# The first batch of a fused attention-and-experts kernel: its chain up to the first mixture matmul, reordered over all engines

## The chip, the cores and the metric

The kernel runs on one core of a Trainium2 chip. The metric is the device time of one execution, in microseconds; medians are over several executions. The profile's "span" (first to last instruction) is about 1.8 us shorter than the device time of the same execution. Engines are named as in the profile: PE (TensorE), PEld (its weight loads), DVE (VectorE), ACT (ScalarE), POOL (GpSimd), SP (SyncE, which issues transfers). "Lnnn" is a line of the kernel that is profiled, so the same code has other line numbers before and after.

## The reference

```python
def phi(x):                                   # polynomial sketch, r = 8, x: (4, 4, 1088, 32)
    a = np.einsum('rd,bhsd->bhsr', S1, x)
    b = np.einsum('rd,bhsd->bhsr', S2, x)
    return np.einsum('bhsi,bhsj->bhsij', a, b).reshape(*x.shape[:-1], r * r)
q_p, k_p = phi(q), phi(k)
kv  = np.einsum('bhsf,bhsd->bhfd', k_p, v);  z = k_p.sum(axis=2)
num = np.einsum('bhsf,bhfd->bhsd', q_p, kv)
den = np.einsum('bhsf,bhf->bhs', q_p, z)[..., None] + 1e-06
x   = (num / den).transpose(0, 2, 1, 3).reshape(4352, 128)
# mixture of 4 experts, D = 128, F = 1024
p = domain_probs / (domain_probs.sum(-1, keepdims=True) + 1e-09)
for e in range(4):
    out += p[:, e:e+1] * (np.maximum(x @ w1[e], 0) @ w2[e])
```

S1 and S2 arrive as 64-bit floats, so the kernel decodes them from integer words.

## The kernel before

A batch's keys are turned by DVE (`kT`), projected by PE (`kf`), added and multiplied (`fs`, `kp`), and contracted with v on PE (`kv`). Queries go through `qc`, `qp`, `nd`, `den` to `xT`, the input of the mixture. The mixture is 64 matmuls a chunk: `hp` into `hid` (DVE) into `acc`. Chunks of later batches are prepared in pieces that are laid between mixture steps; only the first chunk has nothing to hide behind. I call the time until the first `hp` the front, and the rest the main part.

```python
# S: 8 small loads, half of them on ACT, into a tile that GpSimd zeroes
nc.gpsimd.memset(s_raw[:, :], 0)
for i, src in enumerate((S1, S2)):
    for c in range(4):
        (nc.sync if i == 0 else nc.scalar).dma_start(...)
kn[0] = load_rows(k, 0, "kn")
...                                    # dp on ACT
vn[0] = load_v(0, (nc.sync, nc.scalar))
qn[0] = load_rows(q, 0, "qn")
...
nc.vector.memset(warm[:, :], 0.0)
for _ in range(10):                    # warm-up matmuls, PE only
    nc.tensor.matmul(wp[:, :], warm[:, 0:P], warm[:, :], start=True, stop=True)
...                                    # decode of S on DVE, 19 operations and a transpose; sk, sq by one operation each

def keys(b):                           # the same code for every batch
    ...
    for h in range(H):
        for x in range(2):
            eng = nc.vector if b == 0 else nc.gpsimd
            eng.tensor_tensor(out=_ap(kp, ...), in0=..., in1=..., op=ALU.mult)
    ...
    for p in range(2):
        for t in range(NT):            # 66 columns: this pair's two heads
            nc.tensor.matmul(kv[:, WP * p : WP * p + WP], kp[0:n, t, p, :],
                             ve[0:n, t, 2 * p : 2 * p + 2].rearrange("p h d -> p (h d)"), ...)

pieces = front()
while not ready:                       # the first chunk's keys, then its queries, one after the other
    next(pieces)
```

## Time and profile before

| | before |
|---|---|
| median device time (4 runs) | 550.57 us (550.18 to 550.66) |
| profiled execution | 548.74 us, span 546.9 us |
| first hp | 30.03 us |
| from the first hp to the end | 516.9 us |
| PE busy | 530.9 us (97%) |

The lines behind this are shown in the prediction. An fp32 matmul appears as two passes, so "kv x36" is 18 matmuls.

### The profile page before, as it was taken

The page shows a single profiled execution, that of the slowest core. Times are in us where ns is not written, and L with a number is a line of the kernel's source. Part 1 is how long each engine was busy: PE and PEld are TensorE (multiplying, and loading weights), DVE is VectorE, ACT ScalarE, POOL GpSimd, SP SyncE. Part 2 cuts the span into 40 slices and gives each one's busy share as a digit, 9 for nine tenths or more (in the row PEclk, how much of TensorE's full clock was granted, in tenths as well). Part 3 has the DMA queues.
Part 4 walks back from the last instruction along what each step waited for, and adds up shares of the span by engine and source line. Part 5 has one row for each costly group of instructions (what it writes and reads, how often), then busy time and mean ns, then how long its engine had stood idle before and what let it go on. Part 6 is the DMA issues. An engine that isn't in the chain of part 4 may idle for free.

```text
span 546.9 us, 5467 instructions
## 1 busy us (share of the span) xinstructions
PE 530.9 (97%) x2102; PEld 370.1 (68%) x2102; DVE 335.3 (61%) x799; ACT 19.5 (4%) x41; POOL 29.4 (5%) x104
## 2 busy tenths in 40 slices
PE   5689999999999999999999999999999999999997
PEld 3578888776676556666766556675667665565997
DVE  6478875377776745357875664437776654554554
ACT  1000000000000000000000000000000000000000
POOL 2100002400000002400000000400000000000000
PEclk8579999999999999999999999999999999999999
DMA  6870412001105102000201000200200100100100
GB/s 192 253 235 0 128 51 68 1 0 29 42 1 141 43 0 73 0 0 1 73 0 56 5 1 1 71 1 0 72 1 0 43 0 0 35 0 0 16 7 7
DMA packets 32970, 22.54 MB, mean 41 GB/s; under 512 B 21296, under 2 KB 29616, under 8 KB 32944
## 3 DMA queue, kind: packets, MB, share of 16 engines
q1 hardware_dynamic: 31584, 21.79, 14.2%
q10 hardware_dynamic: 1360, 0.41, 0.3%
q8 instruction: 16, 0.26, 0.2%
q14 instruction: 10, 0.08, 0.1%
HBM read 19.88 MB, written 2.31 MB: 41 GB/s over the span
## 4 chain that ended last, share of the span: by engine, by line
PE 95%; DVE 3%; issue 0%; DMA 0%; ACTq 0%; ACT 0%; POOL 0%; DVEq 0%; POOLq 0%
PE hp L406 43%; PE acc L422 43%; PE kv L301 4%; PE nd L359 3%; PE qc L331 2%; PE kf L269 1%; DVE den L372 1%; DVE kp L287 0%; DMA s_raw<-in_S_dram 0%; DVE kT L241 0%; ACTq L101 0%; DVE qp L347 0%; DVE fs L274 0%; DVE hid L408 0%; DVE qa L344 0%
## 5 line engine op out<-in xcount | busy, mean ns | idle before, releaser
L408 DVE SCALAR_TENSOR_TENSOR hid<-hp,gate 128x384 f32<-128x384 f32 (+4 forms) x448 | 213.0, 476 | 193.7 <-PE hp L406 189.0
L406 PE MATMUL hp<-xT,w_sb 128*128 128x384 f32 (+4 forms) x896 | 310.1, 428 | 2.9 <-DVE xT L377 2.7
L422 PE MATMUL acc<-hid,w_sb 128*128 128x384 f32 (+4 forms) x896 | 307.7, 425 | 0.0
L406 PEld LDWEIGHTS hp<-xT,w_sb 128*128 128x128 f32 x896 | 165.0, 191 | 75.2 <-DVE xT L377 3.3
L422 PEld LDWEIGHTS acc<-hid,w_sb 128*128 128x128 f32 x896 | 166.1, 190 | 72.9
L287 POOL TENSOR_TENSOR kp<-fs 128x128 f32<-128x128 f32 (+1 forms) x48 | 19.0, 436 | 315.3 <-DVE fs L274 315.3
L372 DVE RECIPROCAL den<-den 128x128 f32<-128x128 f32 (+1 forms) x37 | 32.3, 875 | 1.8 <-ACT den L362 1.8
L347 DVE TENSOR_TENSOR qp<-qa,qb 64x384 f32<-64x384 f32 (+4 forms) x56 | 26.6, 474 | 1.1
L362 ACT ACTIVATE den<-nd,eps 64x384 f32<-64x384 f32 (+4 forms) x28 | 14.4, 515 | 348.6 <-PE nd L359 348.1
L301 PEld LDWEIGHTS kv<-vx,kp 128*128 128x128 f32 x144 | 19.7, 208 | 3.9 <-issue 1.8
L301 PE MATMUL kv<-vx,kp 128*128 128x66 f32 x144 | 20.4, 295 | 1.4 <-DVE fs L274 1.3
L359 PE MATMUL nd<-qp,kvz 128*128 128x384 f32 (+4 forms) x56 | 18.2, 445 | 3.1 <-DVE qp L347 3.1
L359 PEld LDWEIGHTS nd<-qp,kvz 128*128 128x128 f32 x56 | 10.6, 199 | 8.7 <-DVE qp L347 3.6
L269 PEld LDWEIGHTS kf<-sk,kT 128*128 128x128 f32 x72 | 10.9, 217 | 6.0 <-DVE kT L241 3.9
L269 PE MATMUL kf<-sk,kT 128*128 128x128 f32 x72 | 11.2, 305 | 3.0 <-DVE kT L241 3.0
L344 DVE STREAM_SHUFFLE qa<-qf 128x384 f32<-128x384 f32 (+4 forms) x28 | 13.9, 497 | 0.0
L377 DVE TENSOR_TENSOR xT<-nd,den 64x384 f32<-64x384 f32 (+4 forms) x28 | 13.3, 473 | 0.5
L331 PE MATMUL qc<-qT,sq 128*128 128x384 f32 (+4 forms) x28 | 10.6, 462 | 1.0 <-DVE qT L327 1.0
L257 POOL COPY vx<-vn 128x128 f32<-128x128 f32 x32 | 8.3, 312 | 10.9 <-DMA vn<-in_v_dram 10.9
L331 PEld LDWEIGHTS qc<-qT,sq 128*128 128x128 f32 x28 | 5.7, 209 | 3.1 <-issue 1.1
L272 ACT COPY fs<-kf 128x256 f32<-128x256 f32 (+1 forms) x12 | 3.8, 319 | 105.4 <-PE kf L269 105.3
L431 DVE STREAM_TRANSPOSE ob<-acc 128x384 f32<-128x384 f32 (+4 forms) x14 | 6.9, 494 | 0.6 <-PE acc L422 0.6
(56 smaller groups left out, 60.8 us busy)
## 6 DMA issues: line engine op xcount, KB each, us to landing
gate<-gates SPq DMA_DIRECT2D x6, 768.0 KB
w_sb<-in_moe_w_dram SPq DMA_DIRECT2D x8, 512.0 KB
gate<-gates SPq DMA_DIRECT2D x4, 640.0 KB
kn<-in_k_dram SPq DMA_DIRECT2D x4, 544.0 KB
qn<-in_q_dram SPq DMA_DIRECT2D x4, 544.0 KB
vn<-in_v_dram SPq DMA_DIRECT2D x28, 64.0 KB
out_dram<-ob SPq DMA_DIRECT2D x24, 48.0 KB
gate<-gates SPq DMA_DIRECT2D x2, 384.0 KB
```

The lines of the kernel that those rows point to most:

```text
L269: nc.tensor.matmul(kf[:, P * t : P * t + P], kT[:, P * (t0 + t) : P * (t0 + t + 1)], sk[:, :], start=True, stop=True)
L287: eng.tensor_tensor(out=_ap(kp, 0, P, 256 * s0 + P * (h // 2) + 64 * x + 32 * (h % 2), [[256, m], [R, 4], [1, R]]), in0=_ap(fs, 0, P, 64 * ...
L301: nc.tensor.matmul(kv[:, WP * p : WP * p + WP], kp[0:n, t, p, :], ve[0:n, t, 2 * p : 2 * p + 2].rearrange("p h d -> p (h d)"), start=(t == 0),
L331: nc.tensor.matmul(qc[:, 0:n], sq[:, :], qT[:, 0:n], start=True, stop=True)
L344: nc.vector.stream_shuffle(in_=qf[:, 0:n], out=qa[:, 0:n], mask=mask_a[x])
L347: nc.vector.tensor_tensor(out=qp[p][64 * x : 64 * x + 64, 0:n], in0=qa[64 * p : 64 * p + 64, 0:n], in1=qb[64 * p : 64 * p + 64, 0:n], op=A ...
L359: nc.tensor.matmul(nd[p][:, 0:n], kvzs[b][:, p, :], qp[p][:, 0:n], start=True, stop=True)
L362: nc.scalar.activation(den[64 * p : 64 * p + 64, 0:n], nd[p][64 - 64 * p : 128 - 64 * p, 0:n], ACTF.Identity, bias=eps[64 * p : 64 * p + 6 ...
L372: nc.vector.reciprocal(den[:, s : s + w], den[:, s : s + w])
L406: nc.tensor.matmul(hp[:, 0:n], w1_sb[:, e, P * f : P * f + P], xT[chunks[m]][:, 0:n], start=True, stop=True)
L408: nc.vector.scalar_tensor_tensor(out=_ap(hid[i], 0, P, 0, [[32, n // 32], [1, 32]]), in0=_ap(hp, 0, P, 0, [[32, n // 32], [1, 32]]), scala ...
L422: nc.tensor.matmul(acc[m][:, 0:n], w2_sb[:, e, f, :], hid.pop(i)[:, 0:n], start=(kk == 0), stop=(kk == NK - 1))
```

## The change

The intent: shorten the front by sharing its work over the idle engines, start the next batch's keys in it, and keep PE's clock up. The core of the diff:

```diff
-    s_raw = cpool.tile([P, 2 * D], I32, name="s_raw")
-    nc.gpsimd.memset(s_raw[:, :], 0)
-    ... 8 loads
+    s_raw = cpool.tile([32, 2 * D], I32, name="s_raw")
+    nc.vector.memset(s_raw[:, :], 0)
+    for i, (eng, src) in enumerate(((nc.scalar, S1), (nc.sync, S2))):
+        eng.dma_start(s_raw[R * i : R * i + R, :], src.bitcast(I32))
 ...
+    load_weights(0)                              # was behind the gates
     nc.vector.memset(warm[:, :], 0.0)
+    nc.scalar.activation(warm[:, 0:1], warm[:, 1:2], ACTF.Identity)
-    for _ in range(10):
+    for _ in range(13):
 ...   # decode: 18 operations and a transpose, ordered so that few wait for their neighbour
+    for h in range(H):
+        (nc.vector.tensor_copy if h % 2 else nc.scalar.copy)(_ap(sk, 32 * h, ...), _ap(s_T, ...))
+        nc.gpsimd.tensor_copy(_ap(sq, 32 * h, ...), _ap(s_T, ...))
 ...   # value copies: GpSimd, 9 pieces -> ACT, 3 pieces; sum of the gates: DVE -> GpSimd
+    def start():
+        for r in range(3): key_turn(0, r)
+        make_gates()
+        qs = queries(0, 0)
+        next(qs)                                 # turn of q
+        kf = [key_project(b, 0)]
+        kf.append(key_project(b, 1))
+        key_add(b, 0, kf[0])
+        for h in range(H):
+            key_product(b, 0, 4, h, 0, nc.vector)
+            key_product(b, 0, 4, h, 1, nc.gpsimd)
+        ...                                      # third kf, adds, store_gates, second products
+        kn[1] = load_rows(k, 1, "kn")
+        load_gate(0, 0)
+        ...
+        for p in range(2):
+            key_sum(b, p, kv, slice(0, H))       # 132 columns: all four heads
+        for _ in range(9): next(qs)              # query products while kv runs
+        key_divide(b, kv, 0, 256 + 2 * (D + 1))
+        ahead = keys(1)
+        next(qs)                                 # nd, den
+        for _ in range(5): next(ahead)           # batch 1: three turns, eight of nine kf
+        for _ in qs: pass                        # reciprocals, xT
+        return ahead
```

## The prediction

> **What bounds the kernel now.** I read the page's shares and slices first, then the chain of waits over the first 45 us, the timeline of the first 45 us, and last the landing records of the transfers. PE is 97% busy, and the chain that ended last is 95% PE. In the chain of waits:
>
> ```profile
> 2.20 1.58 DMA s_raw<-in_S_dram
> ...
> 7.49 0.29 DVE sk L188
> ...
> 11.47 1.70 DVE kp L287 x8
> ...
> 14.85 5.80 PE kv L301 x28
> 20.68 0.49 DVE kvz L313 x2
> ...
> 27.76 1.37 DVE den L372 x2
> ...
> 30.03 1.65 PE hp L406 x4
> ```
>
> (start us, length us, what.) The first mixture matmul starts at 30.03 us. From there to about 543.5 us the PE digits are 9 and the chain is PE without a break except for one stall of some 2 us near 42 us (reciprocals ahead of hid). So two parts: a serial front of 30.03 us, and 513.5 us in which PE is the bound. The change can gain in the front, by moving PE work into it, and hardly anywhere else. The windows view adds the clock of the front (columns: window, PE, PEld, DVE, ACT, POOL busy, PEclk, DMA share, GB/s):
>
> ```profile
> 15.00:20.00 5.00, 5.00 (x27) 4.69 (x27) 0.65 (x3) 0.00 (x0) 2.60 (x9) 0.60 0.69 165
> 20.00:25.00 5.00, 1.62 (x5) 0.95 (x4) 3.01 (x14) 0.00 (x0) 0.00 (x0) 0.50 0.99 328
> 25.00:30.00 5.00, 1.65 (x4) 1.14 (x4) 2.98 (x7) 0.83 (x2) 0.00 (x0) 0.50 1.03 359
> 30.00:35.00 5.00, 4.97 (x21) 4.79 (x22) 2.96 (x11) 0.00 (x0) 0.00 (x0) 0.69 1.14 333
> ```
>
> PE runs at half clock from 16.0 to 33.1 us, through most of kv, nd and the first hp, although kv kept it "busy" 5.00 of 5 us. A later batch's kv at full clock shows the difference: 18 passes in 2.10 us (117 ns each), against 28 in 5.80 us (207 ns each).
>
> ```profile
> 103.51 2.10 PE kv L301 x18
> ```
>
> The timeline shows what ACT does before its first copy:
>
> ```profile
> 1.19 4.45 PE L137 MATMUL wp<-warm 128*128 128x512 bf16 x10 [1.19 <-DVE warm L116]
> 6.56 1.53 ACTq L88 DMA_DIRECT2D vn<-in_v_dram  x2
> 8.13 1.28 ACT L272 ACT_TABLE_LOAD   x1 [8.13 <-DMA vn<-in_v_dram]
> ```
>
> ACT's queue is held until 8.1 us by v loads that wait for earlier transfers; the table load comes only then. Today nobody notices: its first copy is wanted at 10.3.
>
> **What the Trainium skill says.** "TensorE: Matmul & The Clock Gate", Part 1: the array runs at half rate until a free-running activity window of about 3.4 us was busy, and falls back after an idle one. The trace agrees: its clock records change in steps of 3.413 us. kv at half clock did not count as busy, which fits 66 columns streaming only half of each 207 ns pass (192 columns take 162 ns at full clock, so 66 take 56, and 112 at half). The same Part 1 ("Architectural detail") says ACT and DVE are strict FIFO; the trace agrees, the table load following the last issue at once. "ScalarE: Activation LUTs", What ACT_TABLE_LOAD costs, gives about 1283 ns; the trace has 1283. "GPSIMD Engine Reference", Engine selection, has GpSimd about 2 times slower on two-input work; the trace has 408 ns for a 128x128 kp product there and 1.70/8 = 213 ns on DVE.
>
> **The change, part by part.**
>
> S and the decode. S comes in 2 transfers instead of 8, zeroed by DVE rather than GpSimd. I estimate landing at 2.5 us (the first of the old ones: issued 0.91, landed 2.28) instead of 3.78. The decode is 18 operations in an order where few wait for their neighbour (about 0.10 us apart, as independent ones are now; dependent ones are 0.21 apart) plus transpose: about 2.4 us instead of 3.5. s_T is ready near 5.1 instead of 7.4. kn goes out 0.9 us earlier and lands near 5.7 (now 6.54); kT is ready by 7.3 instead of 9.3.
>
> But this gain is not kept. In the built instruction order ACT has its loads first, then the table load, then a dummy activation that writes one column of the warm tile, then two of the four sk copies. The v loads wait as they do now, 0.9 us earlier: the last issue at 6.85 to 7.2, table load to 8.5, dummy to 8.7, sk to 9.2. And the first warm-up weight load waits for ACT, since it reads the tile that the dummy writes. So the warm-ups, which began at 1.19, begin at 8.75 and stand ahead of kf in PE's order. There are 13: 0.427 us each at half clock (their spacing now), half of that at full, and full comes 2 to 5.4 us later depending on the window's phase, say 3.7. 3.7/0.427 = 8.7 slow ones and 4.3 fast: 4.6 us. **kf starts near 13.4 us, not 8.66.** That is the wait that takes the place of the decode.
>
> From there PE is warm, and everything is shorter. kf: 16 passes at 111 ns (8 took 0.885 warm in a later batch) end at 15.2, with ACT copies of 0.37 and DVE adds of 0.38 behind. Products: half on DVE (4 x 0.213, 4 x 0.246), half on GpSimd (4 x 0.408, 4 x 0.464): adds done 16.8, pt 17.2, DVE's products 18.2, GpSimd's 18.9. The value copies move to ACT in 3 pieces, about 1.6 us, done 17.7. kv starts at 17.0 and does 36 passes; 132 columns at full clock stream 112 ns, so a pass still costs about 115 ns, and PE counts as busy: ends 21.4 with the waits (now 13.65 to 20.64). The query shuffles and products (22.62 to 25.59 now, 3.0 us) run on DVE during kv instead of after it: ready at 21.2. kvz to 22.0, nd 0.65 us.
>
> Then a new piece: DVE turns batch 1's keys (0.69 + 0.69 + 0.2) before the reciprocals. They need kn of batch 1, whose load stands behind the four gates stores on SP; those need pt (17.2) and take 1.8 us to issue. kn is issued at 19.0 and lands 3.6 us later at about 22.6 (estimate from kn's 4.2 now beside other loads). Turns end 24.1, reciprocals 1.37, xT 0.74: **first hp at about 26.2**, 3.8 us earlier. The gate tile follows kn and lands near 24; weights 0 were loaded long before.
>
> Main part. 16 of batch 1's kf passes now run in the front, while DVE does reciprocals: 16 x 0.111 = 1.8 us off PE. If hp starts at full clock, the half-speed start is spared: from 30.03 to 33.17 PE did 1.4 us worth of full-clock work, so up to 1.7; I count 0.9, since it is about even whether the window before hp (kf of batch 1 alone, 1.8 of 3.4 us) holds the clock. DVE has three more adds in the first chunk, where it has little slack: +0.5. The other batches do the same work, with copies on ACT instead of GpSimd, off the path: 0.
>
> Sum: -3.8 - 1.8 - 0.9 + 0.5 = -6.0. I shade this by 0.5 because DVE and GpSimd now multiply at the same time in one memory. **550.5 - 5.5 = 545.0 us.**
>
> **The rivals.**
> 1. The clock falls back before or in kv. For it: gaps near 16 us while PE waits for products. Against: 132 columns, and kf just before. Then kv takes 36 x 0.22 = 7.9 us instead of 4.4, nd 1.7, hp starts cold: 549 to 551, no gain.
> 2. The order of ACT does not hurt: the warm-ups run early, or full clock comes at once. Then kf starts at 9.3 to 12.5 and hp near 23 to 25: 541 to 543. The waits in the built order speak against the first form; the phase allows part of the second.
> 3. A transfer becomes the bound: kn of batch 1 or the gate tile, behind the gates stores, lands 2 to 3 us later than I think. hp near 28.5: 547.
> 4. Giving back in the main part: ACT's value copies block den, or DVE stalls hid more in the first chunk: +1 to +3. Against it: after 45 us PE waits almost nowhere now, and the order after the first chunk is nearly the old one.
>
> **Range and chances.** The phase of the window alone moves the front by -0.9 to +0.9 us and the clock rival by +4; transfers +2; a quicker ACT -3. So 541.5 to 549.0, 8 in 10. Two per cent is 11.0 us: below 539.5 needs hp to start by about 21 us; I give it 0.03. Slower by 11 us needs something broken in the main part: 0.01.
>
> **What would show it.** Right: in the new timeline the table load at 7 to 8.5 on ACT, the warm-ups only after it, the first kf 4 to 5 us later than before; PEclk near 1 through kv; kv passes near 115 ns; DVE waiting for a kn transfer ahead of its turn; hp first at 25 to 27.5 us; 8 kf pairs ahead of it. Wrong: warm-ups at 1 us; PEclk 0.5 through kv; the first hp before 24 or after 28.5; or the time from first hp to the end differing from 513.5 - 2.2 by over 2 us.

## The result

| | before | after |
|---|---|---|
| median device time (4 runs each) | 550.57 us (550.18 to 550.66) | 543.91 us (543.14 to 544.39) |
| profiled span | 546.9 us | 542.6 us |
| first hp | 30.03 us | 28.65 us |
| from the first hp to the end | 516.9 us | 514.0 us |

The ratio is 0.9879 (95% interval 0.9862 to 0.9896). Ratios here are the mean time of one kernel's fast runs over that of the other's of the same rounds, so not quite the ratio of the medians. The change is faster by 1.2%, inside the 2% that counts as the same.

The chain of waits of the changed kernel over the front (start us, length us, what):

```profile
2.45 4.69 DMA vn<-in_v_dram
...
7.16 0.33 ACTq L88
...
9.07 5.73 PE wp L141 x13
14.80 1.07 PE kf L266 x8
...
16.30 0.44 DVE fs L274
...
24.26 0.50 DVE kvz L307 x2
...
28.65 0.61 PE hp L485 x2
```

S and its decode are gone from the chain. In their place stand a load of v that ACT must wait for before it may issue its last one, and then the warm-up matmuls. From the first key add (16.30) to kvz (24.76) the chain is DVE without a gap, and kv is no longer in it; after that come nd on PE, den on ACT, and the reciprocals and xT on DVE. (The piece "kf" begins with kf's second pass. The first, at 14.59, follows the last warm-up; I take first passes where I give kf's start.)

ACT's timeline of the changed kernel (start us, busy us, engine, line, what; in brackets the wait before it):

```profile
5.75 1.74 ACTq L88 DMA_DIRECT2D vn<-in_v_dram  x2
7.51 1.28 ACT L119 ACT_TABLE_LOAD   x1 [7.51 <-DVE dsum L209]
8.81 0.21 ACT L119 ACTIVATE warm<-warm 128x1 bf16<-128x1 bf16 x1
8.92 0.42 ACT L188 COPY sk<-s_T 32x32 f32<-32x32 f32 x2
```

The table load starts 0.02 us after the last issue ended (7.16 + 0.33 = 7.49), so it is the queue and not "DVE dsum" that held it; the name in brackets is the last semaphore event seen, and the table load waits for none. The warm-ups, at 9.07 in the chain above, start 0.05 us after the dummy activation ends (8.81 + 0.21 = 9.02), and kf follows the last warm-up.

The windows view of the changed kernel, with the same columns as in the prediction:

```profile
15.00:20.00 5.00, 3.44 (x28) 3.12 (x26) 3.67 (x11) 2.23 (x6) 2.92 (x7) 1.00 0.01 2
20.00:25.00 5.00, 4.29 (x32) 3.67 (x31) 4.79 (x18) 0.00 (x0) 0.79 (x2) 1.00 0.68 205
25.00:30.00 5.00, 3.42 (x24) 2.93 (x23) 3.88 (x10) 1.58 (x4) 0.00 (x0) 1.00 0.57 115
30.00:35.00 5.00, 4.98 (x30) 4.93 (x31) 3.51 (x13) 1.55 (x4) 4.96 (x13) 1.00 0.96 272
```

PEclk is 1.00 from 15.02 us on, when kf had begun. (It is printed as 1.00 before that as well, but the trace's first clock record is at 15.02 us, and all 13 warm-ups ran 0.427 us apart, that is at half clock: in a_kp_dve below, where the clock rose among them, the last ones are 0.216 us apart.) In the timeline kv's 36 passes take 4.92 us, 0.112 us apart for the most part, against 0.213 us at half clock in the kernel before:

```profile
16.76 1.53 DVE L282 TENSOR_TENSOR kp<-fs 128x128 f32<-128x128 f32 x4
16.80 1.75 POOL L282 TENSOR_TENSOR kp<-fs 128x128 f32<-128x128 f32 x4 [8.87 <-DVE fs L274]
...
18.83 1.96 POOL L282 TENSOR_TENSOR kp<-fs 128x160 f32<-128x160 f32 x4 [0.28 <-DVE fs L274]
18.93 2.04 DVE L282 TENSOR_TENSOR kp<-fs 128x160 f32<-128x160 f32 x4
...
19.17 4.92 PE L294 MATMUL kv<-vx,kp 128*128 128x132 f32 x36
```

A DVE product took 1.53/4 = 382 ns here against 213 ns before: beside each other, the two engines got through one product each per 0.411 us.

### The profile page after: what moved, and what is told of

Its sections match the earlier page's. It is cut to its first block, busy times and chain, and to the rows that moved or that the text cites. A ratio compares the mean times of both kernels' runs of the same rounds, so it can differ in the third digit from the quotient of the medians.

```text
span 542.6 us, 5443 instructions
## 1 busy us (share of the span) xinstructions
PE 525.9 (97%) x2105; PEld 366.1 (67%) x2105; DVE 333.2 (61%) x788; ACT 25.3 (5%) x56; POOL 26.1 (5%) x80
## 4 chain that ended last, share of the span: by engine, by line
PE 95%; DVE 3%; DMA 1%; issue 0%; ACT 0%; ACTq 0%; DVEq 0%
PE hp L485 43%; PE acc L501 43%; PE nd L381 3%; PE kv L294 2%; PE qc L353 1%; PE wp L141 1%; PE kf L266 1%; DMA vn<-in_v_dram 1%; DVE kp L282 1%; DVE den L394 1%; DVE qp L369 0%; DVE fs L274 0%; DVE hid L487 0%; ACT den L384 0%; DVE qa L366 0%
## 5 line engine op out<-in xcount | busy, mean ns | idle before, releaser
L282 POOL TENSOR_TENSOR kp<-fs 128x128 f32<-128x128 f32 (+1 forms) x56 | 22.6, 442 | 316.4 <-DVE fs L274 316.4
L294 PEld LDWEIGHTS kv<-vx,kp 128*128 128x128 f32 x144 | 17.9, 190 | 2.2
L294 PE MATMUL kv<-vx,kp 128*128 128x66 f32 (+1 forms) x144 | 18.5, 277 | 0.0
L141 PE MATMUL wp<-warm 128*128 128x512 bf16 x13 | 5.7, 632 | 9.1 <-ACT warm L119 9.1
L266 PEld LDWEIGHTS kf<-sk,kT 128*128 128x128 f32 x72 | 9.8, 197 | 3.0 <-DVE fs L274 0.8
L266 PE MATMUL kf<-sk,kT 128*128 128x128 f32 x72 | 10.0, 281 | 0.6 <-DVE fs L274 0.5
L141 PEld LDWEIGHTS <-warm 128*128 128x128 bf16 x13 | 1.8, 146 | 12.1 <-ACT warm L119 9.1
L349 DVE STREAM_TRANSPOSE qT<-qn 128x384 f32<-128x384 f32 (+4 forms) x14 | 6.9, 493 | 3.9 <-DMA qn<-in_q_dram 3.9
```

The source lines that it names most:

```text
L266: nc.tensor.matmul(kf[:, P * t : P * t + P], kT[:, P * (t0 + t) : P * (t0 + t + 1)], sk[:, :], start=True, stop=True)
L282: eng.tensor_tensor(out=_ap(kps[b], 0, P, 256 * t0 + P * (h // 2) + 64 * x + 32 * (h % 2), [[256, n], [R, 4], [1, R]]), in0=_ap(fss[b], 0, ...
L294: nc.tensor.matmul(kv[:, 256 * p : 256 * p + heads.stop * (D + 1) - heads.start * (D + 1)], kps[b][0:n, t, p, :], ve[0:n, t, heads].rearra ...
```

## The experiments

Twelve runs were made, all correct; two are of the kernel before and one of the changed kernel, unchanged. The table gives their medians, the kernel before in the same rounds, the ratio, and from the profiled execution the first hp and the time from there to the end of the span. "Clock" is the mean granted clock of the profiled execution; it counts the time before the trace's first clock record as full, so the 1.000 of the changed kernel leaves out its warm-ups at half clock. The change's other parts (value copies on ACT, gate sums on GpSimd, S in two loads) had no run of their own.

| run | us | before | ratio | first hp | hp to end | clock |
|---|---|---|---|---|---|---|
| changed kernel, first measured | 543.91 | 550.57 | 0.9879 | 28.65 | 514.0 | 1.000 |
| b_again | 549.77 | 551.36 | 0.9983 | 29.46 | 517.6 | 0.983 |
| a_kv66 | 546.17 | 551.36 | 0.9908 | 30.65 | 514.1 | 0.989 |
| b_kv132 | 549.08 | 551.36 | 0.9954 | 27.98 | 517.3 | 0.986 |
| a_warm_free | 540.74 | 551.36 | 0.9808 | 23.93 | 513.9 | 0.997 |
| a_old_decode | 543.95 | 550.39 | 0.9894 | 28.11 | 513.9 | 1.000 |
| a_kp_dve | 543.36 | 550.39 | 0.9881 | 27.14 | 514.0 | 1.000 |
| a_no_ahead | 546.70 | 550.39 | 0.9945 | 27.19 | 517.4 | 0.994 |
| c_early_act | 536.97 | 550.39 | 0.9771 | 20.92 | 513.9 | 1.000 |
| a_again | 543.29 | 550.46 | 0.9864 | 28.53 | 514.0 | 1.000 |
| b_look | 550.17 | 550.46 | – | 31.34 | 517.1 | 0.978 |
| a_warm8 | 542.71 | 550.46 | 0.9853 | 27.18 | 513.9 | 0.999 |
| d_qc_mid | 540.44 | 550.46 | 0.9811 | 24.01 | 515.6 | 0.991 |

The column "hp to end" is the most useful one: it has a floor of 513.9 to 514.1 us, whatever the front took, and each excess over it goes with one or both of two things, told below: batch 1's kf in the main part, and half clock at its start.

**The kernel before against itself.** No edit.

> The kernel before, unchanged, to see its own spread. Its profiled run took 548.74 us, its timed runs 550.2 to 550.7; the changed kernel's profiled run lies inside its timed ones. Theory: the phase of PE's activity window differs from run to run, and one more window of 3.41 us at half clock in the front or at the start of the mixture costs up to 1.7 us. Then the runs fall on two or three levels about 1.7 us apart, and the mean granted clock of a run is lower where the time is longer (548.7 went with 0.981; 550.5 should go with about 0.975 to 0.978). Rival: the gap is something else (launch, DMA), and time and clock are unrelated.

Six executions took 548.68, 548.68, 548.85, 550.68, 551.23 and 552.46 us, with clocks of 0.981, 0.981, 0.983, 0.974, 0.975 and 0.972. The order by clock is nearly the order by time, as the theory of the window's phase says, though the levels are not clean steps of 1.7 us, and the two short traces are out of order (17.1 us at half clock with a span of 547.1 us here, 20.5 us with 546.9 us in the first profile). (Three of the eleven runs of the kernel before beside them report clock 1.000 with 551.7 to 552.0 us; since the first clock records of a trace can be missing, as above, I make nothing of those.) So a single profile of this kernel is known only to some 3 us. The later look shows what a typical run is like:

> The kernel before once more for its trace, since both traces so far are of its short runs (546.9 and 547.1 us, clock 0.981 and 0.983), while its timed runs have spans of 547 to 550.7. Theory of the window's phase: a trace of span 548.6 or more shows half clock for longer (20 us at 0.972 to 0.978: 24 to 30 us at half), the first hp at 30 to 32 us or half clock for 2 to 3 us more after it, and the same 515.5 to 517.5 from hp on otherwise. If this one is short again, the question stays with the clock figures of the timed runs.

This run took 550.17 us (a single execution, so its state is unknown). Its chain of waits:

```profile
16.29 5.67 PE kv L301 x28
...
26.95 1.66 PE nd L359 x4
...
31.34 1.65 PE hp L406 x4
```

Its clock records show half speed from 7.4 to 14.2 and from 17.6 to 34.7 us. The first hp came at 31.34 us and the rest took 517.1 us, as in the other two traces of this kernel. The theory holds in this trace; the profile that I had predicted from was one of the kernel's short executions.

**kv's width, both ways.**

```diff
 # a_kv66: the changed kernel
-            key_sum(b, p, kv, slice(0, H))
+            key_sum(b, p, kv, slice(2 * p, 2 * p + 2))
-        key_divide(b, kv, 0, 256 + 2 * (D + 1))
+        key_divide(b, kv, 0, 256)
```

> The changed kernel with only kv of the first batch put back to 66 columns a pass. Clock theory: at full clock a 66-column pass streams 56 of 117 ns, so PE no longer counts as busy during kv, the clock falls to half for one window or more around kv and nd, and the first hp starts later or cold: +1 to +4 us, to 545 to 548, mean clock below 1.0. Rival (the front is bound by DVE from the first key add to kvz, with no gap, and kv is beside it; kf and qc keep PE busy enough): within 0.5 us of 543.9, clock 1.0.

546.17 us. Chain and windows of this run:

```profile
18.82 6.41 PE kv L294 x36
...
30.86 0.63 PE hp L485 x2
```

```profile
20.00:25.00 5.00, 5.00 (x27) 4.74 (x25) 3.53 (x14) 0.00 (x0) 0.28 (x1) 0.61 0.77 234
25.00:30.00 5.00, 4.42 (x19) 4.23 (x19) 3.76 (x9) 1.21 (x3) 0.00 (x0) 0.50 0.46 82
```

With 66 columns the clock fell at 21.1 us, in the middle of kv, and stayed at half until 31.3. kv was back in the chain, and nd took 1.65 us instead of 0.61. (The first hp pass is at 30.65; the chain's piece begins with the second.) All four executions had a clock of 0.989 to 0.991. The rival, that kv's width does not matter because kv lies beside DVE's chain, is refuted: without the width the median is some 2 us longer.

```diff
 # b_kv132: the kernel before, first batch only
-                    kv[:, WP * p : WP * p + WP],
+                    kv[:, 256 * p : 256 * p + KW],            # KW = 2 * WP for b == 0
-                    ve[0:n, t, 2 * p : 2 * p + 2]...
+                    ve[0:n, t, (slice(0, H) if b == 0 else slice(2 * p, 2 * p + 2))]...
 ...   # and kvz reads kv at the new places
```

> The kernel before with only kv of its first batch widened to all heads. Clock theory: kv was the bound of the old front (5.0 us in which DVE waited for it) because the clock fell to half in it; with 132 columns the clock stays or comes back: kv 4.2 to 5 us instead of 7.0, and the first hp starts at full clock: -3 to -5 us, 545.5 to 547.5. Rival: a full-width pass at half clock streams 224 ns, longer than the 207 ns of now, and the clock does not come back in time: 0 to +1 us.

549.08 us, a ratio of 0.9954: about half of what I expected. kv itself went as the theory says, 28 passes in 3.99 us:

```profile
15.02 3.99 PE kv L302 x28
...
23.58 1.66 PE nd L360 x4
...
27.98 1.65 PE hp L407 x4
```

But then PE had only the query projection to do while DVE worked through the queries, and the clock fell again at 21.7 us and stayed at half until 31.9, so nd and the start of the mixture were slow as before (517.3 us from hp on). Width keeps the clock only while kv runs; it is the rest of the order that carries it to the mixture.

**The warm-ups' wait for ACT.**

```diff
 # a_warm_free: the changed kernel
-    nc.scalar.activation(warm[:, 0:1], warm[:, 1:2], ACTF.Identity)
+    dummy = cpool.tile([P, 2], F32, name="dummy")
+    nc.vector.memset(dummy[:, :], 0.0)
+    nc.scalar.activation(dummy[:, 0:1], dummy[:, 1:2], ACTF.Identity)
```

> The changed kernel with the dummy activation on a tile of its own, so that the warm-up matmuls no longer wait for ACT. ACT's own order is left, so sk is still ready only at 9.35 us. My step: the warm-ups tied to ACT cost the front what the decode gained. Then warm-ups run at about 1.2 to 6.7, kf starts at 9.4 instead of 14.8, the first key add is held by the turn of q in front of it on DVE until 11.75 (now 16.3), so up to 4.5 us are gained if the clock holds: 539.5 to 541. Rival: the late warm-ups are what keeps the clock; with them early PE goes into kf and kv at half clock (kf 3.7, kv 8 us) and the gain is mostly lost: 543 to 546, mean clock 0.97 to 0.985.

540.74 us. The first key add came at 11.70 us, held by the load of q as foreseen, and the first hp at 23.93 instead of 28.65:

```profile
6.93 4.37 DMA qn<-in_q_dram
11.32 0.38 DVE qT L351
...
23.93 0.61 PE hp L487 x2
```

The clock dipped for one window (8.9 to 12.3 us, while kf ran) and came back. So the tie between warm-ups and ACT costs the changed kernel about 3 us net: it does let kf run at full clock (0.112 us a pass, against 0.213 here), but that is worth less than the wait.

**The decode.** In place of the new 18 operations, the old 19 in the old order, on 32 partitions. (The expectation says 22, which counts the transpose and the making of sk and sq too.)

```diff
 # a_old_decode: the changed kernel
-    expo = bits("expo", high, 1, shl, 21, shr)
-    sign = bits("sign", high, 31, shr, 31, shl)
-    ...
+    sign = bits("sign", high, 31, shr, 31, shl)
+    expo = bits("expo", high, 1, shl, 21, shr)
+    mant = either("mant", bits("mant0", high, 12, shl, 9, shr), bits("mant1", low, 29, shr))
+    ...
```

> The changed kernel with the old decode of S (22 operations in the old order, on 32 partitions). My step: the decode is no longer on the path, since sk waits for ACT until 9.3 us and kf for the warm-ups until 14.8; so s_T comes about 1.2 us later (5.8 instead of 4.6), kT about 1 us later (8.2 instead of 7.2), and nothing else moves: first hp within 0.3 us of 28.65, time within 0.5 us of 543.9. Rival: the shorter decode is part of the gain: +0.8 to +1.2 us.

543.95 us. The transposed S was ready 1.2 us later (its transpose starts at 5.58 instead of 4.38), the keys' turn followed (6.39 instead of 5.75), and the warm-ups and kf did not notice: the first hp at 28.11. The faster decode is worth nothing in this order that these runs can resolve.

**The split of the products.**

```diff
 # a_kp_dve: the changed kernel
-            key_product(b, 0, 4, h, 1, nc.gpsimd)
+            key_product(b, 0, 4, h, 1, nc.vector)
 # and the same for the second group
```

> The changed kernel with all key products of the first batch on DVE, none on GpSimd. Theory: DVE and GpSimd slow each other, so that the half share on DVE (4 in 1.53 us, 4 in 2.04) took almost as long as all eight do alone (1.70 and 1.97 before): products then take 3.7 us instead of 3.5 to 3.6, the front hardly moves (-0.1 to +0.4 us): 543.8 to 544.5. Rival: the DVE products are slow for a reason of their own (the order, the waits) and not because GpSimd runs beside: then eight at 0.38 and 0.51 us take 7.1 us, +3.5 us.

543.36 us. All eight products on DVE took about as long as four did beside GpSimd:

```profile
15.19 1.71 DVE L282 TENSOR_TENSOR kp<-fs 128x128 f32<-128x128 f32 x8
...
17.54 1.93 DVE L282 TENSOR_TENSOR kp<-fs 128x160 f32<-128x160 f32 x8
```

That is 214 and 241 ns each, against 382 and 510 ns in the changed kernel. From the first key add to the end of kvz it is 8.5 us here (14.73 to 23.24) and 8.5 us there (16.30 to 24.75). The rival, that DVE was slow for a reason of its own, would have given 7 us of products; they took 3.6. Sharing them moved work off DVE without moving its end. (The 0.5 us in the median's favour goes with shorter warm-ups, 4.37 us in this profile; from the first key add to hp it is 12.4 us in both kernels.)

**Batch 1's keys in the front.**

```diff
 # a_no_ahead: the changed kernel
-        for _ in range(5):
-            next(ahead)
 ...
-        for _ in range(3):
+        for _ in range(8):
             next(ahead)
             yield
```

> The changed kernel without the five pieces of batch 1's keys (three turns, eight kf) in the front; they come as the first pieces of the mixture. Theory: those pieces are free in the front (they lie in the shadow of ACT's den and of the reciprocals) and take 1.8 us of PE off the mixture: without them +1.8 us, and +0.5 to 1.5 more because DVE is tight in the first chunk: 545.7 to 547.5; first hp at most 0.3 us earlier. Rival: they delay the reciprocals and so cost the front what they save: within 0.5 us of 543.9.

546.70 us. The front was no shorter for it: from the first key add (14.78) to hp (27.19) it took 12.4 us, as in the changed kernel (16.30 to 28.65). The main part took 517.4 us, 3.4 us over the floor. Of these, 16 passes at 111 ns = 1.8 us are batch 1's kf (an estimate). The rest, which I had put down to DVE beforehand, goes with the clock. The windows view:

```profile
25.00:30.00 5.00, 2.81 (x8) 2.49 (x9) 3.69 (x9) 0.00 (x0) 0.00 (x0) 0.55 0.72 185
30.00:35.00 5.00, 5.00 (x30) 5.00 (x30) 1.36 (x6) 0.74 (x2) 0.00 (x0) 0.76 1.05 328
```

Without kf between nd and hp, PE idles for 3 us there, and the mixture starts at half clock, which lasted from 25.5 to 32.4 us. So batch 1's keys in the front are worth 1.8 us as work, and the remaining 1.6 us go with the clock that they hold; no run separates the two further.

**The number of warm-ups.**

```diff
 # a_warm8: the changed kernel
-    for _ in range(13):
+    for _ in range(8):
```

> The changed kernel with 8 warm-up matmuls instead of 13. My step: the warm-ups stand in the way of kf. Then kf starts after 8 x 0.427 = 3.4 us of them, at 12.5 instead of 13.4 to 14.8, and the first hp comes 0.9 to 2.3 us earlier: 541.7 to 543 if kf and kv get full clock soon enough. Rival: 13 are needed for the clock; with 8 the clock rises one window later or falls in the gap before kv, kf takes 3.4 us and kv up to 8: 544 to 548, mean clock below 1.

542.71 us against 543.29 for the changed kernel on the same chip, which ran beside it as follows.

> The changed kernel, unchanged, beside the last variants on one chip. 543.1 to 544.6 us. Its front depends on when full clock comes within the warm-ups (5.73 us of them in the first profile, 4.33 to 5.7 in the variants), so its runs should lie within 1.5 us, and the first hp at 27.1 to 28.7; from the first hp to the end 513.9 us.

Its four runs took 543.06 to 544.26 us. With 8 warm-ups kf started at 12.48 instead of 14.69 us, at half clock, so its first eight passes were 0.213 us apart instead of 0.112; the first hp came 1.35 us earlier in the profiles and the medians differ by 0.6. This is a small gain at the edge of what the spread allows; it agrees in sign with the warm-ups standing in kf's way, and the clock, full from 14.70 us on, did not need all 13.

**ACT out of the way.** This version came out of the above: the dummy activation on its own tile and ahead of ACT's v loads, all sk copies on DVE, and q's turn behind the key adds.

```diff
 # c_early_act: the changed kernel
+    dummy = ...; nc.vector.memset(dummy[:, :], 0.0)
+    nc.scalar.activation(dummy[:, 0:1], dummy[:, 1:2], ACTF.Identity)   # behind the load of dp
 ...
-    nc.scalar.activation(warm[:, 0:1], warm[:, 1:2], ACTF.Identity)
 ...
-        (nc.vector.tensor_copy if h % 2 else nc.scalar.copy)(
+        nc.vector.tensor_copy(
 ...
-        next(qs)                        # in front of the first kf
 ...
         store_gates()
+        next(qs)
```

> The changed kernel with ACT out of the way of the start: the dummy activation on a tile of its own and ahead of ACT's v loads, so that the table load runs at about 2 us; all four sk copies on DVE; the turn of q behind the key adds on DVE. Theory: the front is then warm-ups to 6.7, kf, and DVE's chain of about 8 us from the first key add (now at about 8.4 to 9.5) to kvz, then 4.4 us to hp: first hp at 20.7 to 22.5, time 536.5 to 539, if clock and the kn and gate transfers (kn of batch 1 at about 16.5) allow it. Rivals: the clock falls to half between kf and kv (kv 8 us): 540 to 542, mean clock 0.985 to 0.99; or the later v loads on ACT hold kv or the fs copies: 539 to 541.

536.97 us, ratio 0.9771 (0.9750 to 0.9791): the only run that is faster than the kernel before by the 2% that count. Against the changed kernel's 0.9879 it is 1.1% better, clear of both intervals. ACT's timeline and the chain of waits:

```profile
1.99 1.28 ACT L106 ACT_TABLE_LOAD   x1 [1.99 <-DVE warm L121]
2.06 1.34 ACTq L83 DMA_DIRECT2D vn<-in_v_dram  x3
```

```profile
1.26 5.36 PE wp L143 x13
6.62 1.14 PE kf L268 x8
...
11.86 4.65 PE kv L296 x36
...
20.92 0.61 PE hp L487 x2
```

The table load runs while ACT's queue goes on issuing loads: a running instruction does not stop the queue, but a load that waits in the queue stops everything behind it. kf starts at 6.62, behind the warm-ups and the first turn of the keys, the first hp at 20.92, and the main part takes the floor's 513.9 us. The gain over the changed kernel lies wholly in the front.

```diff
 # d_qc_mid: c_early_act
+        key_sum(b, 0, kv, slice(0, H))
         next(qs)
         next(qs)
-        for p in range(2):
-            key_sum(b, p, kv, slice(0, H))
+        key_sum(b, 1, kv, slice(0, H))
```

> The kernel with ACT out of the way of the start (which took 536.97 us), with the query projection between kv's two halves instead of in front of them. There kv began at 11.86 behind the query projection, which waited for the turn of q; kvz waited 0.4 us for kv. Theory: kv's first half starts at 10.0 to 10.5, kvz is bound by DVE alone: 0.4 us earlier, 536.3 to 537. Rival: the projection now comes late for DVE's shuffles (wanted at 12.8) because kv's first half waits for GpSimd's products: +0.3 to +1 us.

A miss: 540.44 us, and neither theory had it. Its clock records show half speed from 12.1 to 18.9 us and again from 25.8 to 29.2; the last 10 passes of kv's first half took 2.77 us and the 18 of its second half 3.86 us, and the main part 515.6 us, 1.7 us over the floor with nothing else moved there. All four runs had a clock below 1 (0.991 to 0.997), and three of four of c_early_act's had 1.000.

The records narrow it down. For each window of 3.41 us at full clock one can estimate from the matmul records how long columns streamed through PE (192 columns take 0.162 us). In the windows before d_qc_mid's two falls that is 1.18 and 1.26 us, before b_again's at 16.9 it is 1.29, before a_kv66's 1.39. In the trace of c_early_act, whose clock held, the least is 1.42, and in the first 36 us of these fourteen traces no window after which the clock held has less than 1.40. The view's busy time does not sort them: b_again's window was busy for 3.06 us, all of it 66-column passes of kv, and the clock fell; c_early_act's from 9.52 to 12.93 was busy for 1.63 and it held. So the moved projection did leave two windows with too little streaming here. Whether it would at every phase of the window, no run shows; this part stays open.

## Why the prediction was right

The range held (545.0 predicted, 543.9 measured), but the total is nearer than its parts: that is in part luck, as the steps show. The prediction's own signs were mixed. As named for "right": the table load, the warm-ups behind it, PEclk and kv's passes (0.112 us), eight kf pairs ahead of hp, and a main part within 2 us of the sum. Not so: kf 5.9 us later than before instead of 4 to 5, no wait of DVE for kn, and a first hp at 28.65, just beyond the 28.5 that it had named as a sign of being wrong. By its own steps:

- **What bounds it: right.** A front and a PE-bound main part. The main part can be shortened only by work taken out or by the clock: every run has 513.9 to 514.1 us there, plus 1.8 us where batch 1's kf is in it, plus 1.2 to 1.9 us where half clock falls into its start (d_qc_mid alone shows the second, with 1.7; the kernel before and a_no_ahead have both, and there the parts are worked out by difference).
- **The decode's gain is not kept: right**, and shown by a_old_decode. The numbers of the step were close: table load 7.51 to 8.79 (predicted 7.2 to 8.5), sk at 9.34 (9.2), warm-ups from 9.07 (8.75).
- **kf near 13.4: mis-sized.** It started at 14.59 in the first profile, since all 13 warm-ups ran at half clock (5.5 us to kf's first pass, predicted 4.6): full clock came 5.95 us after the first of them, where 3.7 was counted and 2 to 5.4 allowed. Other traces of the same order had 4.33 to 5.7 us, so the estimate was within the spread of the window's phase, and this profile at its long end.
- **Products on two engines: the term that failed.** "4 x 0.213, 4 x 0.246" on DVE is 1.84 us; they took 1.53 + 2.04 = 3.6. I set aside 0.5 us for the two engines in one memory; it was about 1.7. So the products ended at 20.97 instead of 18.2 and kvz at 24.75 instead of 22.0. a_kp_dve shows the mechanism: sharing the products with GpSimd, the step's purpose, gained nothing.
- **kv at full clock, 132 columns counting as busy: right**, and shown in both directions by a_kv66 and, for kv alone, b_kv132. kv left the chain.
- **The wait for batch 1's keys: did not come.** The load was issued at 20.85, as late as feared, and landed at 24.57; but DVE reached the turn only at 24.66, because of the products. It is a near tie.
- **First hp at 26.2: it was 28.65**, from 1.2 us up to kf's start and 1.6 from there to the end of the products, less 0.3 for the keys that were in time.
- **Main part, -2.2 us: it was -2.9** against the profile of before. Batch 1's kf, which I called even odds for holding the clock, does hold it: without it, in a_no_ahead, the clock fell at 25.5 us. For the clock and DVE's adds together I had counted -0.4; it is -1.1 here, once the 1.8 of kf is taken off, and -1.6 by a_no_ahead. No run tells the two apart.
- **A base that was off.** I took differences from a profile of 548.7 us and subtracted them from a median of 550.5. A typical run of the kernel before starts its mixture near 31.3 us and not at 30.0 (b_look, one trace, close to the medians in its time). So the front gained about 3 us in typical runs (31.34 to 28.53 in the two profiles of one chip) and the main part 3.1: together 5.9 of the 6.7 us between the medians, the rest being the spread of the changed kernel's own runs (its profiled ones were its longest). The total came out near because the too large gain in the front was matched by a base that was too short: this is luck. From profile to profile the gain was 4.3 us (546.9 to 542.6), where 5.5 was foreseen.
- **What the parts are worth.** Taken out of the changed kernel one at a time, kv's width is worth 2.3 us between medians (546.17 and 543.91, of different rounds) and batch 1's keys in the front 2.8; the new decode and the split of the products are worth nothing that shows.
- **Two readings to put right.** The 207 ns of a kv pass "at half clock" average a few passes before 16.0 us in; from 16.8 us on they are 213 ns apart. And 408 ns is how long one GpSimd product lasts; they start 0.364 us apart in batch 1, so four take 1.5 us and not 1.63.
- **The rivals.** The clock's fall (1) is what happens with 66 columns, not with 132. ACT's order (2) hurts, as argued: a_warm_free took the warm-ups' wait for it away and gained 3 us. The transfers (3) were not the bound. Giving back in the main part (4) did not occur.

## What to carry to other kernels

Before counting the gain of a shorter step, follow the in-order queues of the built program: a dummy activation meant to load a table early sat behind waiting loads on ACT, and through the tile that it touched it held PE's warm-ups, and with them everything; moving it, together with two copies and a turn, took the median from 543.9 to 537.0 us (ratios to the kernel before of 0.9879 and 0.9771). Splitting elementwise work between DVE and GpSimd can leave DVE no sooner finished. Where PE has a free-running activity clock, compare several executions' clocks before taking differences of a microsecond from one profile, and give PE useful work in every gap of the front.

## What the Trainium skill lacked or had wrong

- "GPSIMD Engine Reference", Specifications, says that GpSimd contends with DVE instructions that have two SBUF inputs, but gives no size; "SBUF — State Buffer", Summary, has the second to issue fully blocked until the first finishes. Here the products of the two engines alternated, one of each per 0.411 us, where with no such product on the other engine GpSimd started one every 0.364 us (batch 1) and DVE one every 0.202 us (a_kp_dve): slower than either, and faster than the 0.566 us of strict turns (an estimate, their sum). A DVE product of 128x128 took 382 ns beside GpSimd and 214 ns alone (128x160: 510 and 241). DVE bears most of it.
- "ScalarE: Activation LUTs", What ACT_TABLE_LOAD costs, adds a drain of about 1380 ns to the load's 1283 ns for a switch. The load took 1.28 us here, but the first activation started at 8.81, 0.02 us after it ended; no such drain shows for the first load of a program. No run here switches between sets.
- "TensorE: Matmul & The Clock Gate", Part 1, says that a busy window brings full clock, but not what counts as busy. A row of matmuls without a gap is not enough: in the kernel before PE was busy 5.00 of 5 us between 15 and 20 us, with 66-column fp32 passes 213 ns apart from 16.8 us on, and the clock stayed at half. The clearest pair is at half clock: 66-column passes 213 ns apart filled a window of a_kv66 (21.07 to 24.48) and the clock did not rise; 132-column passes 220 ns apart filled one of d_qc_mid (15.52 to 18.94) and it rose.
- The same Part 1 calls the penalty of the ramp less than 1% and advises against fitting it. For a change of 1.2% what goes with it is no longer small, over half of the effect: one unchanged kernel ran from 548.68 to 552.46 us with clocks from 0.983 to 0.972.
